# Float16 parts of q and k for the scores of two batches, in a kernel of attention and two expert layers

## The chip, the cores and the metric

The kernel runs on one core of a Trainium2 chip. The metric is the time of one execution on the device, in microseconds (us); less is better. The core has five engines that run side by side, each through a list of instructions in order: TensorE (PE, matrix products; its weight loads are shown apart as PEld), VectorE (DVE), ScalarE (ACT), GpSimd (POOL) and SyncE (SP), which here issues the transfers (DMA).

## The reference

Attention over 4 batches, 8 heads, 576 tokens and 64 dimensions of a head, with a retrieval from a memory beside it, then two layers of the form in-product, pointwise function, out-product. Everything is float32.

```python
scores = scale * np.matmul(q, k.transpose(0, 1, 3, 2))        # scale = 1/8
scores = np.where(causal, -1000000000.0, scores)
a = np.exp(scores - scores.max(-1, keepdims=True))
a /= a.sum(-1, keepdims=True) + 1e-09
local = np.matmul(a, v)
mem_out = (phi(q) @ M_prev) / (phi(q) @ z_prev + 1e-06)        # phi(x) = x + 1, or exp(x) for x < 0
x = g * mem_out + (1 - g) * local                              # g = sigmoid(beta), one for each head
...                                                            # x is laid out as 2304 tokens x 512
y   = (s * relu(x @ w_in)**2 + b) @ w_out                      # layer 1, d_ff = 2048
h   = y @ w_in2
out = (max(h, 0) + alpha * min(h, 0)) @ w_out2                 # layer 2, d_ff = 2048
```

## The kernel before

**Attention.** The work is cut into units, a unit being two heads (a pair) of one batch: 4 pairs for each of batches 0, 2 and 3, and 8 half units in batch 1 (SPLIT). The 576 queries are cut into five chunks of 128, 128, 128, 128 and 64 (CHUNKS, AT). The scores of chunk c against its keys are one matmul for each head (L974), of 256, 384, 128, 512 and 576 columns; the two heads of a pair lie in the upper and the lower 64 partitions, so that two matmuls of 64 rows each fill the array. Batches 0, 2 and 3 (QUAD) issue the scores of a unit in two steps: chunks 0 and 1, and then 2, 3 and 4. The float32 q and k are the operands directly, with no preparation. `largest` (L947) adds the mask and takes the maximum of a row, `exps` (L940) takes the exponent with its sum, and the weights go turned into the output products, in float16 parts for batches 1 to 3 (L878). `values` makes two float16 parts of v in each unit, scaled by a sum that is taken over it: Abs with an accumulator (L672), a reduction on GpSimd (L675), small operations on VectorE, a scaled copy on ScalarE (L684), a subtraction on VectorE (L686). L918 puts the unit's result together, L1035 sends it to the memory `x1`.

**Layer 1.** Tokens are taken in blocks: block 0 has 512, blocks 1 to 7 have 256. The x of a block is loaded in halves of two pairs (L1195), cast to the format of the products on ScalarE (L1202) and its rest taken on VectorE (L1204). A block of 256 goes in 16 steps of 24 matmuls: `g1` makes the hidden values of 128 columns of w_in in 12 matmuls into the bank `hb` (L1109 to L1111), ScalarE and VectorE square them (L1122 to L1125), and `g2` adds their share of the output in 12 matmuls into `yb` (L1143 to L1145). `x` and the weights are in two parts each, so there are three products. L1179 stores y. While layer 1 goes on, the weights of layer 2 are prepared: L1263 to L1278 combine them, L1314 and L1317 split them into float16 parts on ScalarE and VectorE, and L1409, L1410 and L1460 do the like with y.

**Layer 2** uses seven products in place of eight with such parts (L1485 to L1487 and L1624 to L1626).

**What sets the order.** Nothing is issued as the code stands. Each piece is an `op` with an engine, an assumed cost, the pieces that it needs and a priority; the class Plan simulates the engines and, whenever one is free, lets it take the ready piece of the lowest number. Attention has numbers from 0 on (`ATT`), the layers from 10,000,000 on (`MOE`), so that layer matmuls fill what attention leaves of TensorE. The table NUDGE shifts the number of single pieces. In the program that comes out, each engine goes through its list strictly in order.

Of the kernel before, what the change touches and what calls it, by code (L numbers as in the profile page):

```python
# [10 lines left out]
FP16 = mybir.dt.float16  # L11
# [38 lines left out]
GW = 640  # L50
# [16 lines left out]
LIFT = 2.0 ** 14  # L67
TOP, DOWN = 2.0 ** 13, 2.0 ** -22
WP = 1.7
NUDGE = {  # L70
# [391 lines left out]


def t_p(ns):

    return 206 + 4 * sum(ns) / 2.4 + (0, 0, 4, 160, 187)[len(ns)]


def t_dve(n, rate=1.04, extra=0.0):
    return 69 + n * rate + extra  # L470


def t_act(n, fixed=93.0, extra=0.0):
    return fixed + n * 0.834 + extra
# [1256 lines left out]
```

## Time and profile before

| what | value |
|---|---|
| median of three runs | 907.01 us (906.0 to 907.03) |
| the profiled execution | 904.36 us |
| its span, from the first to the last instruction shown | 902.6 us |
| mean granted clock of TensorE | 0.998 |
| TensorE busy | 889.4 us, 99% of the span |
| VectorE busy | 748.6 us, 83% |
| ScalarE busy | 608.4 us, 67% |
| GpSimd busy | 13.9 us, 2% |

The span is what the profiler sees of the profiled execution; 1.76 us of it lie outside. Busy time is the union of an engine's instructions. Matmuls overlap one another in their pipeline, so the distance from one start to the next says what a matmul costs, and its duration does not.

### The profile page before, as it was taken

How to read it: one execution, taken by the hardware profiler on the slowest of the kernel's cores; microseconds unless marked ns; L12 is line 12 of the kernel's file. 1: busy time of each engine (PE TensorE's matmuls, PEld its weight loads, DVE VectorE, ACT ScalarE, POOL GpSimd, SP SyncE). 2: the span in 40 equal slices, each digit the busy share in tenths (PEclk: the TensorE clock that was granted, in tenths of full speed). 3: DMA queues.
4: the chain of work that ended last, by engine and by line, in shares of the span. 5: the costliest groups of instructions: out<-in, count | busy, mean ns of one | idle time of the engine just before them, and what ended most of it. 6: DMA issues, size and time to landing. Idle time of an engine off the chain costs nothing.

```text
span 902.6 us, 19354 instructions
## 1 busy us (share of the span) xinstructions
PE 889.4 (99%) x7144; PEld 690.7 (77%) x7144; DVE 748.6 (83%) x1729; ACT 608.4 (67%) x1416; POOL 13.9 (2%) x41
## 2 busy tenths in 40 slices
PE   8999999999999999999999999999999999999998
PEld 5767678688988898899999999765566666666665
DVE  8999999788686757759988978898968899795974
ACT  8987776788788878744545478876758775455451
POOL 0000000000000000000000000000000000000000
PEclk9999999999999999999999999999999999999999
DMA  4359895387957586457878769856544262726202
GB/s 164 110 167 261 194 283 184 75 233 123 151 135 158 122 188 116 95 185 254 297 253 279 263 221 325 277 187 216 170 163 169 105 201 99 245 88 191 89 1 70
DMA packets 154527, 160.44 MB, mean 178 GB/s; under 512 B 86976, under 2 KB 128576, under 8 KB 154432
## 3 DMA queue, kind: packets, MB, share of 16 engines
q1 hardware_dynamic: 154144, 158.91, 60.0%
q8 instruction: 56, 0.92, 0.4%
q14 instruction: 39, 0.32, 0.1%
q10 hardware_dynamic: 288, 0.30, 0.1%
HBM read 92.84 MB, written 46.66 MB: 155 GB/s over the span
## 4 chain that ended last, share of the span: by engine, by line
PE 84%; DVE 9%; DMA 3%; ACT 2%; issue 1%; SPq 0%; DVEq 0%
PE yb L1143 7%; PE hb L1109 7%; PE yb L1145 7%; PE yb L1144 6%; PE hb L1111 6%; PE hb L1110 6%; PE sp L1626 3%; PE sp L1625 3%; PE sp L1624 3%; PE yb L1626 3%; PE yb L1625 3%; PE yb L1624 3%; PE sp L974 2%; PE yb L1487 2%; PE yb L1486 2%; PE yb L1485 2%
## 5 line engine op out<-in xcount | busy, mean ns | idle before, releaser
L1109 PE MATMUL hb<-xr,wt 128*128 128x256 f32 (+1 forms) x512 | 152.8, 299 | 1.1 <-ACT gt L1122 1.1
L1143 PE MATMUL yb<-gr,wt 128*128 128x256 f32 (+2 forms) x512 | 153.4, 300 | 0.2
L1145 PE MATMUL yb<-gr,wt 128*128 128x256 f32 (+2 forms) x512 | 150.7, 294 | 0.7 <-DVE gr L1125 0.5
L1111 PE MATMUL hb<-xr,wt 128*128 128x256 f32 (+1 forms) x512 | 149.7, 292 | 0.4 <-DVE wt L1075 0.4
L1110 PE MATMUL hb<-xr,wt 128*128 128x256 f32 (+1 forms) x512 | 149.4, 292 | 0.0
L1122 ACT ACTIVATE gt<-hb 128x256 f32<-128x256 f32 (+1 forms) x128 | 52.4, 410 | 97.5 <-PE hb L1111 93.7
L1109 PEld LDWEIGHTS hb<-xr,wt 128*128 128x128 f32 x512 | 96.5, 189 | 11.1 <-issue 5.6
L1143 PEld LDWEIGHTS yb<-gr,wt 128*128 128x128 f32 x512 | 96.6, 189 | 9.4 <-issue 5.1
L1145 PEld LDWEIGHTS yb<-gr,wt 128*128 128x128 f32 x512 | 96.4, 188 | 4.5 <-DVE gr L1125 1.9
L1111 PEld LDWEIGHTS hb<-xr,wt 128*128 128x128 f32 x512 | 96.2, 188 | 3.8 <-DVE wt L1075 1.4
L1110 PEld LDWEIGHTS hb<-xr,wt 128*128 128x128 f32 x512 | 96.2, 188 | 2.3
L1144 PE MATMUL yb<-gr,wt 128*128 128x256 f32 (+2 forms) x320 | 93.7, 293 | 0.0
L1125 DVE TENSOR_TENSOR gr<-gt,gr 128x256 fp32r<-128x256 f32 (+1 forms) x128 | 58.2, 455 | 31.2 <-ACT gr L1124 29.9
L1144 PEld LDWEIGHTS yb<-gr,wt 128*128 128x128 f32 x320 | 60.2, 188 | 1.4
L1124 ACT CAST gr<-gt 128x256 fp32r<-128x256 f32 (+1 forms) x128 | 55.2, 431 | 6.0 <-PE yb L1144 3.5
L1123 ACT ACTIVATE gt<-gt 128x256 f32<-128x256 f32 (+1 forms) x128 | 56.8, 444 | 2.4
L1144 PE MATMUL yb<-gr,wu 128*128 128x256 f32 (+2 forms) x192 | 56.2, 293 | 0.0
L1486 PEld LDWEIGHTS <-wp 128*128 128x128 f16 x336 | 32.9, 98 | 23.0 <-issue 1.6
L1625 PEld LDWEIGHTS <-wp 128*128 128x128 f16 x336 | 32.9, 98 | 21.7
L1626 PEld LDWEIGHTS <-wp 128*128 128x128 f16 x336 | 32.9, 98 | 21.7
L1624 PEld LDWEIGHTS <-wp 128*128 128x128 f16 x336 | 32.9, 98 | 21.7
L1487 PEld LDWEIGHTS <-wp 128*128 128x128 f16 x336 | 32.9, 98 | 21.7
(493 smaller groups left out, 2427.6 us busy)
## 6 DMA issues: line engine op xcount, KB each, us to landing
g<-poolx SPq DMA_DIRECT2D x96, 192.0 KB, 1.9
poolu<-g SPq DMA_DIRECT2D x30, 384.0 KB, 4.4
pool<-wout SPq DMA_DIRECT2D x13, 512.0 KB, 4.9
room<-win SPq DMA_DIRECT2D x13, 512.0 KB, 4.3
room<-wout SPq DMA_DIRECT2D x12, 512.0 KB, 4.1
pool<-win SPq DMA_DIRECT2D x11, 512.0 KB, 4.8
spare<-y SPq DMA_DIRECT2D x12, 384.0 KB, 4.1
spare<-g SPq DMA_DIRECT2D x12, 384.0 KB, 3.8
```

The source lines that it names most:

```text
L1109: T.matmul(H_, W_h, X_h, start=(d == 0), stop=False)
L1110: T.matmul(H_, W_h, X_l, start=False, stop=False)
L1111: T.matmul(H_, W_l, X_h, start=False, stop=(d == KD - 1))
L1123: op("ACT", t_act(n), lambda: A.activation(out=t_, in_=t_, func=AF.Square), w=[tk], prio=-1)
L1124: op("ACT", t_act(n), lambda: A.copy(out=G_h, in_=t_), r=[tk], w=[("gh", gj)], prio=-1)
L1125: op("DVE", t_dve(n), lambda: V.tensor_tensor(out=G_l, in0=t_, in1=G_h.bitcast(F32), op=ALU.subtract), r=[tk, ("gh", gj)], w=[("gl", gj)], ...
L1143: T.matmul(Y, W_h, G_h, start=first, stop=False, skip_group_check=True)
L1144: T.matmul(Y, W_l, G_h, start=False, stop=False, skip_group_check=True)
L1145: T.matmul(Y, W_h, G_l, start=False, stop=False, skip_group_check=True)
L1624: T.matmul(o, W_h, G_h, start=(m == e == 0 and P in (1, 2, 4, 5)), stop=False, skip_group_check=True)
L1625: T.matmul(o, W_l, G_h, start=False, stop=False, skip_group_check=True)
L1626: T.matmul(o, W_h, G_l, start=False, stop=False, skip_group_check=True)
```

## The change

Batches 2 and 3 (HALF) take their scores from float16 parts. `halves` makes, once for each unit, a scale for q and one for k from the sums of their absolute values (largest over the partitions), and a high and a low part of each. `mm16` then has three matmuls in place of one: high by high, high by low, low by high, into the same bank. The scores come out scaled; `exps` takes the scale back by the factor of its activation, and `unscale`, a small operation behind `largest`, by a product with the row's maximum. The mask's constant becomes larger. `t_h` is the cost that Plan assumes for the new score steps. All of NUDGE is listed anew, since the numbers of the pieces behind the new ones shift.

```diff
+HALF = (2, 3)
 NUDGE = {
-    0: 45, 1: 61, 5: 2, 6: -161, 8: -3, 10: 90, 12: 1, 15: 111, 16: 376, 17: -48, 18: -27, 19: -30, 20: -37, 22: 3,
...
+    4422: 46, 4423: 46,
 }
+def t_h(ns):
+
+    return 150 + 3 * sum(n / 2.4 + 3 for n in ns) + 100 * (len(ns) > 2)
...
+        hst = stat[:, 98:116].rearrange("p (a b) -> p a b", a=2)
...
-            V.tensor_scalar(out=mask[:, S - 128:], in0=col, scalar1=row[:, 0:1], scalar2=-8.0e9, op0=ALU.is_gt, op1=ALU.mult)
+            V.tensor_scalar(out=mask[:, S - 128:], in0=col, scalar1=row[:, 0:1], scalar2=-1.0e30, op0=ALU.is_gt, op1=ALU.mult)
...
+        def halves(u, sq, sk, ranges):
+
+            j = u % 2
+            x = hst[:, j]
+            out = [Slot(RES["vf"]) for _ in range(2)]
+            for e, (s, o, (a, z)) in enumerate(zip((sq, sk), out, ranges)):
+                op("ACT", t_act(z - a, 93, 180), lambda e=e, s=s, o=o, a=a, z=z: A.activation(
+                    out=at(o, S)[:, a:z], in_=at(s, ranges[1][1] if e else S)[:, a:z], func=AF.Abs, accum_out=x[:, e:e + 1]),
+                   r=[s], w=[o, ("hm", j, e)])
+            op("POOL", 900, lambda: nc.gpsimd.partition_all_reduce(x[:, 2:4], x[:, 0:2], 128, ReduceOp.max),
+               r=[("hm", j, e) for e in range(2)], w=[("hx", j)])
+
+            def scales():
+                V.tensor_scalar(out=x[:, 4:6], in0=x[:, 2:4], scalar1=2.0 ** -15, scalar2=2.0 ** -15, op0=ALU.max, op1=ALU.mult)
+                V.reciprocal(out=x[:, 6:8], in_=x[:, 4:6])
+                V.tensor_scalar(out=x[:, 8:9], in0=x[:, 4:5], scalar1=x[:, 5:6], scalar2=-1.0, op0=ALU.mult, op1=ALU.mult)
...
+                op("ACT", t_act(z - a, 93, 93), lambda part=part, raw=raw, sc=sc: A.activation(
+                    out=part(0), in_=raw(), func=AF.Copy, scale=sc), r=[s, ("hs16", j)], w=[o])
+                op("DVE", t_dve(z - a, 1.04, 60), lambda part=part, raw=raw, sc=sc: V.scalar_tensor_tensor(
+                    out=part(1), in0=raw(), scalar=sc, in1=part(0), op0=ALU.mult, op1=ALU.subtract), r=[s, ("hs16", j)], w=[o])
+            return out
...
-                        out=at(s, GW)[:, x + k0:x + k0 + kn], in_=bank_at(bk)[:, at0:at0 + kn], func=AF.Exp, scale=-1.0, bias=mcol,
+                        out=at(s, GW)[:, x + k0:x + k0 + kn], in_=bank_at(bk)[:, at0:at0 + kn], func=AF.Exp, scale=hst[:, j, 8:9] if b in HALF else -1.0, bias=mcol,
...
+                def unscale(c, cols):
+                    if b not in HALF:
+                        return
+                    m = mx[:, j, cols[0]:cols[-1] + 1]
+                    op("DVE", 73, lambda: V.tensor_scalar(out=m, in0=m, scalar1=hst[:, j, 8:9], scalar2=-1.0, op0=ALU.mult, op1=ALU.mult),
+                       r=[("hs16", j)], w=[("mx", j, x) for x in cols])
...
+                    def mm16():
+                        for y in range(0, len(todo), 2):
+                            for l0, l1 in ((0, 0), (0, 1), (1, 0)):
+                                for bk, rows, odd, q0, nq, k0, n, x in todo[y:y + 2]:
+                                    T.matmul(bank_at(bk)[rows, x:x + n], half16(sq16, odd, l0, q0, nq), half16(sk16, odd, l1, k0, n),
+                                             start=l0 + l1 == 0, stop=l0 == 1, skip_group_check=True)
```

New lines stand between, so the same code has other numbers after: `g1` is L1181 to L1183 and `g2` L1215 to L1217, the layers' work on ScalarE L1194 to L1196, the stores of x and y L1107 and L1251, the loads of x L1267, the scores L1044 (float32) and L1037 (float16), the weight splits L1386 and the copies of y L1532.

Three places of the order show what moves. The first is SyncE at the end of batch 2's attention: the last transfer to `x_65` is the x of pair 3, the loads from it feed a block of layer 1. Before:

```order
L1035 DMA x_65<-pool 128x576
L840 DMA pool<-kp 128x576
L659 DMA pool<-vd 128x640
L1195 DMA poolx<-x_65 128x2x256
L827 DMA_TRANSPOSE pool<-pool 128x10x128 x2
L827 DMA_TRANSPOSE pool<-poolx 128x10x128
L1195 DMA poolx<-x_65 128x2x256
L1179 DMA y_66<-pool 128x256 x2
L1179 DMA y_66<-poolx 128x256
L1179 DMA y_66<-pool 128x256
L1195 DMA poolx<-x_65 128x2x256
```

After:

```order
L1267 DMA poolx<-x_65 128x2x256
L750 DMA poolx<-qp 128x576
L1107 DMA x_65<-pool 128x576
L1251 DMA y_66<-poolx 128x256
L1251 DMA y_66<-pool 128x256 x2
L1251 DMA y_66<-poolx 128x256
L1267 DMA pool<-x_65 128x2x256 x2
L875 DMA_TRANSPOSE pool<-poolx 128x10x128
L875 DMA_TRANSPOSE poolx<-poolx 128x10x128
```

After, the first load stands ahead of that store and belongs to another block; behind the store come four stores of y and then both loads of block 3 together, where before the loads of x lie apart, with loads and transposes of the next units between.

The second is TensorE behind the outputs of batch 2's pair 3 (`yb_103`): before, three layer matmuls and the second score step of the next unit, and then the layer's block goes on (`yb_102`).

```order
L878 MATMUL yb_103<-pool 64x64
L1143 MATMUL yb_101<-gr,wt_1451 128x256
L1144 MATMUL yb_101<-gr,wt_1451 128x256
L1145 MATMUL yb_101<-gr,wt_1451 128x256
L974 MATMUL yb_104<-poolx,pool 128x512
L974 MATMUL sp_106<-poolx,pool 128x512
L974 MATMUL sp_107<-poolx,pool 128x128
L974 MATMUL ob<-poolx,pool 128x128
L974 MATMUL sp_107<-poolx,pool 64x288 x2
L974 MATMUL ob<-poolx,pool 64x288 x2
L1143 MATMUL yb_102<-gr,wt_1451 128x256
L1144 MATMUL yb_102<-gr,wt_1451 128x256
```

After, nine layer matmuls stand there, which end their block, and then the score step in float16 begins, each matmul with its own weight load:

```order
L932 MATMUL yb_103<-pool,poolx 64x64
L1215 MATMUL yb_101<-gr,wt_1756 128x256
L1216 MATMUL yb_101<-gr,wt_1756 128x256
L1217 MATMUL yb_101<-gr,wt_1756 128x256
L1215 MATMUL yb_102<-gr,wt_1756 128x256
L1216 MATMUL yb_102<-gr,wt_1756 128x256
L1217 MATMUL yb_102<-gr,wt_1756 128x256
L1215 MATMUL yb_102<-gr,wt_1756 128x256
L1216 MATMUL yb_102<-gr,wt_1756 128x256
L1217 MATMUL yb_102<-gr,wt_1756 128x256
L1037 LDWEIGHTS pool
L1037 MATMUL sp_106<-pool 128x512
```

Behind that score step, the matmuls of the next block's hidden values (`hb`) begin at once, with none of `yb` between them:

```order
L1037 MATMUL ob<-pool 64x288
L1181 MATMUL hb<-xr,wt_505 128x256
L1182 MATMUL hb<-xr,wt_505 128x256
L1183 MATMUL hb<-xr,wt_505 128x256
L1181 MATMUL hb<-xr,wt_505 128x256
L1182 MATMUL hb<-xr,wt_505 128x256
L1183 MATMUL hb<-xr,wt_505 128x256
L1181 MATMUL hb<-xr,wt_505 128x256
L1182 MATMUL hb<-xr,wt_505 128x256
L1183 MATMUL hb<-xr,wt_505 128x256
L1181 MATMUL hb<-xr,wt_505 128x256
L1182 MATMUL hb<-xr,wt_505 128x256
```

What moved is the start of block 3: it stands 106 layer matmuls behind the outputs before, and 10 to 16 behind them after.

The third is ScalarE near the end of layer 1, where the splits of layer 2's weights (`wp`) and the copies of y (`spare`) stand among the layers' own work (`gt`, `gr`). After:

```order
L1194 ACTIVATE gt<-hb 128x256
L1386 ACTIVATE wp_7065<-wp_7065,stat 128x2x256
L1386 ACTIVATE wp_7167<-wp_7167,stat 128x3x256
L1195 ACTIVATE gt<-gt 128x256
L1532 ACTIVATE spare<-spare,stat 128x384
L1196 CAST gr<-gt 128x256
L1194 ACTIVATE gt<-hb 128x256
L1532 ACTIVATE spare<-spare,stat 128x384
L1195 ACTIVATE gt<-gt 128x256
L1532 ACTIVATE spare<-spare,stat 128x384
L1196 CAST gr<-gt 128x256
L1532 ACTIVATE spare<-spare,stat 128x384
```

The maxima over layer 2's weights (`bounds`), which all splits need, stand at step 114 of layer 1's 128 before and at step 120 after, so that the rows above are among those of the last seven steps.

## Rows read from the trace of the kernel before

**Rows 1.** Busy time by stretch: span, busy us per engine, clock, DMA share, GB/s.
```profile
0.00:60.00 60.00, 54.66 (x484) 39.80 (x486) 55.02 (x222) 53.58 (x166) 2.37 (x12) 0.97 0.45 145
...
180.00:390.00 210.00, 209.82 (x2349) 187.45 (x2351) 153.67 (x495) 168.51 (x475) 5.52 (x18) 1.00 0.69 146
390.00:530.00 140.00, 139.94 (x1252) 139.67 (x1247) 122.30 (x270) 65.56 (x166) 1.34 (x2) 1.00 0.72 252
530.00:570.00 40.00, 39.13 (x328) 37.23 (x327) 32.21 (x58) 35.60 (x72) 0.00 (x0) 1.00 0.93 309
570.00:902.60 332.60, 328.07 (x2025) 198.22 (x2023) 271.88 (x402) 199.81 (x341) 1.03 (x2) 1.00 0.46 150
```

**Rows 2.** TensorE's timeline, a first score step: start us, duration us, instruction.
```profile
266.47 0.48 PE L974 MATMUL yb<-poolx 64*128 64x256 f32 x1
266.47 0.48 PE L974 MATMUL ob<-poolx 64*128 64x256 f32 x1
...
267.75 0.39 PE L1143 MATMUL yb<-gr,wt 128*128 128x256 f32 x1
```

**Rows 3.** TensorE's timeline, the second score step of a unit.
```profile
302.44 0.69 PE L974 MATMUL yb<-poolx,pool 64*128 64x512 f32 x1
...
304.84 0.39 PE L1143 MATMUL yb<-gr,wt 128*128 128x256 f32 x1
```

**Rows 4.** Timelines, x of batch 2's pair 3: TensorE, VectorE, SyncE, ScalarE, VectorE.
```profile
301.90 0.38 PE L1143 MATMUL yb<-gr,wt 128*128 128x256 f32 x1
...
302.03 0.55 DVE L918 TENSOR_SCALAR pool<-yb,vsc 128x320 f32<-128x320 f32 x1 [0.48 <-PE yb L878]
...
302.60 0.33 SPq L1035 DMA_DIRECT2D x<-pool  x1
...
305.95 0.38 SPq L1195 DMA_DIRECT2D poolx<-x  x1
...
310.02 0.71 ACT L1202 CAST xr<-poolx 128x256 fp32r<-128x256 f32 x2
...
311.46 0.73 ACT L672 ACTIVATE pool<-pool 128x640 f32<-128x640 f32 x1
312.09 0.19 ACT L672 ACTIVATION_READ_ACCUMULATOR pool<-pool 128x1 f32 x1
...
310.42 0.88 DVE L686 SCALAR_TENSOR_TENSOR pool<-poolx,vsc,pool 128x640 f16<-128x640 f32 x1
311.22 0.75 DVE L1204 TENSOR_TENSOR xr<-poolx,xr 128x256 fp32r<-128x256 f32 x2
311.89 0.15 DVE L1001 TENSOR_TENSOR sm<-sm 128x1 f32<-128x1 f32 x1
```

**Rows 5.** Busy time by stretch around TensorE's longest wait, columns as in the first.
```profile
50.00:52.00 2.00, 0.61 (x4) 0.21 (x2) 2.00 (x12) 2.00 (x8) 0.00 (x0) 1.00 0.89 250
52.00:54.00 2.00, 1.96 (x9) 1.26 (x11) 1.97 (x9) 1.86 (x7) 0.00 (x0) 0.63 1.01 378
54.00:56.00 2.00, 2.00 (x8) 0.92 (x7) 0.96 (x3) 2.00 (x5) 0.00 (x0) 0.52 1.01 336
```

**Rows 6.** TensorE's timeline, output matmuls in float16.
```profile
197.84 0.22 PE L878 MATMUL sp<-pool,poolx 128*64 128x128 f16 x1
...
197.90 0.22 PE L878 MATMUL sp<-pool,poolx 128*64 128x128 f16 x1
```

**Rows 7.** Page, costliest groups: count, busy us and mean ns, idle before.
```profile
L1486 PEld LDWEIGHTS <-wp 128*128 128x128 f16 x336 | 32.9, 98 | 23.0 <-issue 1.6
```

**Rows 8.** ScalarE by line: count, busy us and mean ns, idle before.
```profile
L1124 ACT CAST gr<-gt 128x256 fp32r<-128x256 f32 (+1 forms) x128 | 55.2, 431 | 6.0 <-PE yb L1144 3.5
...
L1314 ACT ACTIVATE wp<-wp,stat 128x512 f16<-128x512 f32 (+1 forms) x48 | 37.6, 790 | 0.9 <-PE yb L1486 0.5 <-DMA wp<-wdwi 0.2
...
L1460 ACT ACTIVATE spare<-spare,stat 128x384 f32<-128x384 f32 x24 | 16.0, 702 | 0.1
...
L1409 ACT CAST poolu<-spare 128x768 f16<-128x768 f32 x8 | 6.5, 828 | 0.0
```

More of the change, by code (lines that the diff above doesn't have):

```diff
@@ L688, in values, with part, raw @@
             return sf
+        def halves(u, sq, sk, ranges):
[12 more added lines that the diff above has]
+                V.tensor_scalar(out=x[:, 8:9], in0=x[:, 4:5], scalar1=x[:, 5:6], scalar2=-1.0, op0=ALU.mult, op1=ALU.mult)
+            op("DVE", 390, scales, r=[("hx", j)], w=[("hs16", j)])
+            for e, (s, o, (a, z)) in enumerate(zip((sq, sk), out, ranges)):
+                def part(lo, o=o, a=a, z=z):
+                    return at(o, 2 * S, FP16)[:, S * lo + a:S * lo + z]
+                def raw(e=e, s=s, a=a, z=z):
+                    return at(s, ranges[1][1] if e else S)[:, a:z]
+                sc = x[:, 6 + e:7 + e]
+                op("ACT", t_act(z - a, 93, 93), lambda part=part, raw=raw, sc=sc: A.activation(
[3 more added lines that the diff above has]
+            return out
         def features(b, p, u, gs):
@@ L842, in pair, with half16 @@
                    r=gate(b, u, KG), prio=(-21, -8)[k] if b + p == 0 else None, w=[(sk, "b") if k else sk], bytes_=512 * (z - a))
+            if b in HALF:
+                sq16, sk16 = halves(u, sqp, sk, ((AT[SETS[gs[0]][0]], AT[SETS[gs[-1]][-1]] + CHUNKS[SETS[gs[-1]][-1]][0]), (0, nkeys)))
+            def half16(s, odd, lo, x, n):
+                return at(s, 2 * S, FP16)[D * odd:D * odd + D, S * lo + x:S * lo + x + n]
             def half(s, odd, x, n):
@@ L940, in exps @@
                     op("ACT", t_act(kn, 50, 180), lambda: A.activation(
-                        out=at(s, GW)[:, x + k0:x + k0 + kn], in_=bank_at(bk)[:, at0:at0 + kn], func=AF.Exp, scale=-1.0, bias=mcol,
-                        accum_out=scol), r=[(bk, c), ("mx", j, mk)], w=[(s, c, k0), ("sm", j, int(c > 1), col)])
+                        out=at(s, GW)[:, x + k0:x + k0 + kn], in_=bank_at(bk)[:, at0:at0 + kn], func=AF.Exp, scale=hst[:, j, 8:9] if b in HALF else -1.0, bias=mcol,
+                        accum_out=scol), r=[(bk, c), ("mx", j, mk)] + [("hs16", j)] * (b in HALF), w=[(s, c, k0), ("sm", j, int(c > 1), col)])
                     dones[c > 1].append(("sm", j, int(c > 1), col))
@@ L970, in scores @@
                                      for i in range(2) for odd in range(2)]
+                    def mm16():
[4 more added lines that the diff above has]
+                                             start=l0 + l1 == 0, stop=l0 == 1, skip_group_check=True)
                     def mm():
+                        if b in HALF:
+                            return mm16()
                         for bk, rows, odd, q0, nq, k0, n, x in todo:
@@ L980, in scores @@
                         room_for.append(("hs", u))
-                    op("PE", t_p([y[6] for y in todo[::2]]), mm, r=[sqp, sk] + [(s, "b") for s in (sqp, sk) if max(step) > 1],
+                    op("PE", (t_h if b in HALF else t_p)([y[6] for y in todo[::2]]), mm, r=[sq16, sk16] if b in HALF else [sqp, sk] + [(s, "b") for s in (sqp, sk) if max(step) > 1],
                        w=keys + room_for, prio=ATT + (base + 2 * step[0]) * 10, kind="scores")
@@ L991, in pair @@
                         mcols = [largest(c, 2 * c + odd, bks[odd], 0, n, mask[:, S - n:], "mask", at0=at0) for odd in range(2)]
+                        unscale(c, [2 * c, 2 * c + 1])
                         for odd in range(2):
@@ L997, in pair @@
                     m1 = largest(c, 8, bks[1], n2, n2, mask2, "mask2", m0)
+                    unscale(c, [8])
                     exps(c, 0, 9, bks[0], 0, n2, m1, 8)
```

260 rows, old and new, of the table NUDGE are left out of this document.

## The prediction

> **What bounds the kernel now.** I read the busy times by stretch first [rows 1]. TensorE is the bound almost everywhere: 209.82 of 210 us from 180 to 390, 139.94 of 140 up to 530, 39.13 of 40 up to 570, and 328.07 of the last 332.6. Only the first 60 us, in which the attention of batch 0 runs without the layers beside it, are shared: TensorE 54.66, VectorE 55.02, ScalarE 53.58. So a microsecond taken out of TensorE's stream between 180 and 390, where all units of batches 2 and 3 lie, comes off the end, as long as nothing else makes TensorE wait. VectorE (153.67 of 210) and ScalarE (168.51 of 210) have 56 and 41 us to spare there.
>
> Second, TensorE's timeline around the scores [rows 2, 3]. A unit of batches 2 and 3 has two steps of scores. The reader is to see the distance from the first score matmul to the next layer matmul: 267.75 - 266.47 = 1.28 us, and 304.84 - 302.44 = 2.40 us. The eight units repeat this, so the price of scores before is 3.68 us a unit.
>
> Third, how the chain of x is built, since the order puts another neighbour there now (below) [rows 4]. Fourth, the one place where TensorE's clock falls [rows 5].
>
> **The change part by part.**
>
> *Scores.* A unit streams 256 + 384 columns in its first step and 512 + 128 + 2 x 288 in its second, 1,856 for each head, with the two heads side by side (two records of 64 rows start together in [rows 2]). At 2.4 columns per ns, four passes for float32 make 3.09 us, and 0.59 us of the 3.68 are entry, loads and tail. Three float16 products make 3 x 1,856 / 2.4 = 2.32 us. That 128 columns of float16 cost no more than such a stream is seen in the output matmuls, whose pairs start 0.06 us apart [rows 6]; 128 / 2.4 is 0.053. No row shows float16 pairs of 64 rows. I give the entry, the loads and the tail 0.2 to 0.6 us, so 2.5 to 2.9 a unit, a saving of 6.0 to 9.2 us over eight units. I take 2.72, or **-7.7 us**, with the fixed part near the old one. The worst bound is from the weight loads: there are 36 of them in a unit, 98 ns each [rows 7]; if they were strictly one after another and nothing ran under them it would be 3.53 us plus the fixed part, and nothing would be saved. The layers' loads run under the matmuls (187.45 us of loads beside 209.82 of matmuls [rows 1]), so I don't take it.
>
> The Trainium skill ("TensorEngine Tiling (Array Packing)", section "Key Properties") says that different tiles of the array can load weights and multiply in parallel. For float32 the trace agrees as far as multiplying goes: the two heads start within 10 ns. By that rule the short pairs of 128 columns would not wait for two loads in a row, and the saving would be 8.3 us (an estimate); if the loads of the two heads queue it would be 7.2.
>
> *Making the parts.* Each unit gains on ScalarE two Abs with accumulators (0.73 + 0.19) and two scaled copies of about the same 0.73 (these rows are of 640 columns, not 576), about 3.3 us, and on VectorE two subtractions of at most 0.88 and eight small operations of 0.15 to 0.2, about 3.0 us [rows 4]. Eight units make 26 us and 24 us. Spread over 180 to 390 these fit into the 41 and 56 us to spare; operations that may run on either engine can move. POOL's one reduction a unit is nothing to an engine that is busy 5.52 of 210 us [rows 1]. I cost all this at 0 for TensorE, because the parts are made a unit ahead; if that cover were gone, a unit would wait for Abs, reduction, scales, copy, subtraction in a row, some 4 us.
>
> *The order around block 3.* The lists in the order show that the layers reach block 3, whose x needs the attention of batch 2, much closer behind it. Before, the last outputs of batch 2's pair 3 stand at layer matmul 1,035 and block 3's first matmul at 1,141: 106 matmuls between, 106 x 0.112 = 12 us (0.112 is 139.94 us over 1,252 matmuls [rows 1]). After, they stand at 1,143 and 1,153: nine matmuls of the layer's second product (1.01 us), the second score step of the next unit (2.40 x 2.72 / 3.68 = 1.77 us, and 0.2 for the two changes), and six matmuls on the half of x that is there already (0.67): **3.65 us of cover**. What has to happen in that time is seen in the same chain before: the outputs are done and the next layer matmul starts at 301.90; VectorE puts the sum together from 302.03; SyncE sends x away at 302.60 and, when this has landed, loads the block's half at 305.95; ScalarE's cast starts at 310.02 and VectorE's difference at 311.22, of which the first of two is done at about 311.6 [rows 4]. That is 9.7 us. VectorE was at another operation from 310.42 (L686, 0.88 us) while the cast was done, and ScalarE too was between other work, so I let the chain be up to 1.3 us shorter: 8.4. In the order after, x's store is followed on SyncE by four stores of y before the loads, which are issued, not waited for. So TensorE, which stands in order, waits at block 3's seventh matmul for 8.4 - 3.65 = 4.8 to 9.7 - 3.65 = 6.0 us. SyncE's two transposes behind those loads wait with nobody who is late. For what else may differ there I widen it to 4.0 to 6.5 and take **+5.0 us**.
>
> *The clock behind that wait.* In 50 to 52 TensorE is busy 0.61 of 2.0 us, the granted clock then is 0.63 and 0.52 in the next two stretches (1.2 GHz is the lower of its two levels), and full again after it [rows 5]. With about 0.37 + 0.48 of these two stretches of 2 us lost, such a fall costs up to 1.7 us. A wait of 5 us is longer than that one. I take **+1.2** (0 to 1.7).
>
> The Trainium skill ("TensorE: Matmul & The Clock Gate", section "Why this matters for your kernels") warns that gaps between bursts of matmuls let the array drop back to half of its clock. [Rows 5] agree: the clock fell right behind the emptiest stretch. It speaks against this change, which puts a gap into a stretch that had none; without the fall the sum would be 1.2 us lower.
>
> *The end of layer 1.* Preparing the weights of layer 2 starts some steps later and is squeezed into the last seven steps of layer 1. In these the order has on ScalarE 16 weight splits of 0.790, 7 of L1460's copies of 0.702, 3 of L1409's casts of 0.828 and 21 operations of the layers' own of about 0.431 [rows 8]: 12.6 + 4.9 + 2.5 + 9.1 = 29.1 us, less some 0.1 us by which neighbours overlap (311.46 + 0.73 ends 0.1 behind the 312.09 at which the next one starts [rows 4]), 47 x 0.1 = 4.7: 24.4 us. TensorE has 7 x 24 matmuls of 0.112 and 12 products of layer 2 of 0.162 (328.07 us over 2,025 [rows 1]): 20.8 us. So up to 3.6 us could become a wait; before, this stretch loses 0.87 us [rows 1]. ScalarE can run ahead on what doesn't hang on TensorE, so I take **+1.2** (0 to 4).
>
> *The rest.* Up to layer matmul 384 the same work stands in another order: no row prices that, and I put it at 0, with 1.5 us on either side. The mask's constant costs nothing: the same instruction.
>
> Sum: -7.7 + 5.0 + 1.2 + 1.2 = **-0.3 us** on the profiled execution's 904.36, so 904.1. The median of the runs shown is 907.01, 2.65 above that execution; the forecast is 904.1 + 2.65 = 906.7, put as **906.5 us**.
>
> **The rivals.**
>
> *B: the gap isn't there.* If x comes as quickly as the cover allows, the wait and the clock go: -7.7 + 1.2 = -6.5, or 900.5 on the median. For it: ScalarE and VectorE may be freer there than in [rows 4]. Against it: the two transfers alone took from 302.60 to near 310.
>
> *E: the new order wins at the start.* TensorE is idle 5.3 us of the first 60 [rows 1]. If the relisted order closes half of it, 3 us, the sum is -3.3: 903.7. Against: VectorE and ScalarE are nearly full there too, and their work there is the same.
>
> *C, the slower side: ScalarE is overfull in the last seven steps of layer 1.* The layers' relu and square stand behind weight splits on the same queue, and TensorE waits for them. It decides once ScalarE's 24.4 us really run within those steps: 3.6 us of wait in place of 1.2, and a fall of the clock behind them of up to 1.7, so -0.3 + 2.4 + 1.5 = +3.6: 910.6. For it: ScalarE was busy 35.60 of 40 us there already [rows 1]. Against: the splits before it are earlier in the order.
>
> *D: the change doesn't do what it says.* The float16 halves don't run side by side: 3 x 2 x 1,856 / 2.4 = 4.64, with 0.4 fixed 5.04 a unit, 1.36 more than before instead of 0.96 less: -0.3 + 7.7 + 10.9 = +18.3: 925. For it only that no row shows such pairs; against it that float32 ones do run so [rows 2].
>
> **How the numbers follow.** Chances: the forecast 0.40, B 0.18, E 0.15, C 0.22, D 0.05. The forecast's own range is 904 to 909 (saving 6.0 to 9.2, wait 4.0 to 6.5, clock 0 to 1.7). About 0.2%, 1.8 us, is what a measurement of this kernel can tell from no change: faster is below 905.2, slower above 908.8. The forecast gives 0.09 faster, 0.26 same, 0.05 slower; B 0.18 faster; E 0.13 faster and 0.02 same; C 0.05 same and 0.17 slower; D 0.05 slower. Together 0.40, 0.33 and 0.27. The range reaches half a microsecond beyond B's value and C's, 900.0 to 911.0; outside it are D and the far parts of B and C.
>
> **What would show it.** In the profile after: the distance from a unit's first score matmul to the next layer matmul, 2.5 to 2.9 us over both steps; one new wait of 4 to 6.5 us of TensorE at the start of block 3, released by the difference of x, with a granted clock near half in the stretches right behind it; TensorE's idle time from some 20 us before layer 2's stretch to it not above 4 us; TensorE idle about as long in the first 60 us as before. The prediction is wrong if there is no such wait, if the scores take 3.5 us or more, or if a new wait above 2 us stands elsewhere.

## The result, and the profile after

The changed kernel takes 913.12 us (median of 4 runs, 912.83 to 915.95); the kernel before, beside it on the same chip, 906.5. The ratio is 1.0088, with an interval of 1.0065 to 1.0112: slower by 8.0 us, where 906.5 was forecast with a range up to 911.0. The profiled execution took 913.37 us, its span is 911.6.

Busy time by stretch, columns as in [rows 1]:

```profile
0.00:60.00 60.00, 54.61 (x462) 39.14 (x462) 55.19 (x221) 52.32 (x161) 1.43 (x11) 0.97 0.44 138
...
180.00:390.00 210.00, 201.37 (x2272) 181.80 (x2272) 162.35 (x535) 183.70 (x494) 7.56 (x25) 0.98 0.65 138
390.00:530.00 140.00, 139.36 (x1351) 137.91 (x1350) 115.76 (x262) 73.43 (x193) 0.20 (x1) 1.00 0.70 236
530.00:570.00 40.00, 38.42 (x328) 37.45 (x327) 33.36 (x79) 26.65 (x59) 3.56 (x2) 1.00 0.87 300
570.00:911.60 341.60, 337.23 (x2095) 206.10 (x2093) 287.25 (x423) 212.51 (x365) 1.46 (x2) 1.00 0.49 159
```

TensorE stands idle for 210 - 201.37 = 8.63 us from 180 to 390; it was 0.18 in [rows 1]. The loss falls between 175 and 550 us: counted along TensorE's timeline, the 384th layer matmul starts 0.16 us later than before, the 1,728th 9.5, the 2,832nd 7.4 and the 3,000th 8.0.

TensorE's timeline, both score steps of a unit and the start of block 3 (start, duration, line, tiles, count; in brackets the idle time before and what ended it); answers to [rows 2, 3]:

```profile
310.97 0.50 PE L1037 MATMUL sp<-pool 64*128 64x256 f16 x6
311.31 0.32 PE L1037 MATMUL ob<-pool 64*128 64x384 f16 x1
311.31 0.32 PE L1037 MATMUL yb<-pool 64*128 64x384 f16 x1
...
311.88 0.38 PE L1215 MATMUL yb<-gr,wt 128*128 128x256 f32 x1
...
314.54 0.38 PE L1215 MATMUL yb<-gr,wt 128*128 128x256 f32 x1
...
315.77 0.82 PE L1037 MATMUL sp<-pool 64*128 64x512 f16 x6
316.43 0.22 PE L1037 MATMUL yb<-pool 64*128 64x128 f16 x1
316.43 0.22 PE L1037 MATMUL ob<-pool 64*128 64x128 f16 x1
316.48 0.22 PE L1037 MATMUL yb<-pool 64*128 64x128 f16 x1
...
317.54 0.38 PE L1181 MATMUL hb<-xr,wt 128*128 128x256 f32 x1
...
318.23 0.28 PE L1183 MATMUL hb<-xr,wt 128*128 128x256 f32 x1
323.56 0.58 PE L1181 MATMUL hb<-xr,wt 128*128 128x256 f32 x1 [5.05 <-ACT xr L1274]
```

The scores take 311.88 - 310.97 = 0.91 and 317.54 - 315.77 = 1.77 us, 2.68 a unit in place of 3.68. The two heads start at the same time. The wait stands where it was forecast. Its chain in the timelines of the other engines, answering to [rows 4]:

```profile
314.66 0.55 DVE L972 TENSOR_SCALAR pool<-yb,vsc 128x320 f32<-128x320 f32 x1 [0.17 <-PE yb L932]
...
315.24 0.33 SPq L1107 DMA_DIRECT2D x<-pool  x1
315.70 0.33 SPq L1251 DMA_DIRECT2D y<-poolx  x1
316.21 2.48 SPq L1251 DMA_DIRECT2D y<-pool  x2
318.78 0.40 SPq L1251 DMA_DIRECT2D y<-poolx  x1
319.51 0.88 SPq L1267 DMA_DIRECT2D pool<-x  x2
...
322.81 0.70 ACT L1274 CAST xr<-pool 128x256 fp32r<-128x256 f32 x2
```

From the sum on VectorE to TensorE's next matmul it is 323.56 - 314.66 = 8.9 us. (Ahead of the prediction both loads at L1267 are given to block 3. One of the two is the second half of block 3, the other that of block 4.) The clock behind the wait, in stretches of 2 us, answering to [rows 5]:

```profile
318.00:320.00 2.00, 0.51 (x5) 0.30 (x3) 2.00 (x6) 2.00 (x5) 0.00 (x0) 1.00 0.57 189
320.00:322.00 2.00, 0.00 (x0) 0.00 (x0) 2.00 (x9) 1.04 (x4) 0.00 (x0) 0.91 0.68 198
322.00:324.00 2.00, 0.44 (x1) 0.29 (x1) 1.74 (x6) 2.00 (x8) 0.00 (x0) 0.50 1.12 244
324.00:326.00 2.00, 1.49 (x6) 1.14 (x5) 2.00 (x7) 2.00 (x6) 0.00 (x0) 0.50 1.25 176
326.00:328.00 2.00, 1.92 (x9) 1.93 (x10) 0.39 (x4) 2.00 (x9) 0.00 (x0) 0.50 0.99 287
328.00:330.00 2.00, 2.00 (x11) 2.00 (x11) 1.84 (x9) 1.76 (x5) 0.51 (x2) 0.50 0.06 21
330.00:332.00 2.00, 2.00 (x12) 2.00 (x12) 2.00 (x4) 2.00 (x6) 0.00 (x0) 0.53 0.00 0
```

The reader is to see two things: the clock is at half for five stretches, and ScalarE, and but for 326 to 328 (0.39) VectorE, are nearly full in the same ones. Last, the new operations behind the maxima, and two rows of the exponents of 512 columns, the first with the factor read from the tile `stat`, as in batches 2 and 3, the second with a constant (VectorE by line, ScalarE by line and form: count, busy us and mean ns, idle before):

```profile
L1011 DVE TENSOR_SCALAR mx<-mx,stat 128x2 f32<-128x2 f32 (+1 forms) x40 | 8.9, 222 | 0.2
...
L994 ACT ACTIVATE pool<-sp,mx,stat 128x512 f32<-128x512 f32 x7 | 5.4, 776 | 0.0
...
L994 ACT ACTIVATE pool<-sp,mx 128x512 f32<-128x512 f32 x5 | 3.4, 686 | 1.2 <-DVE vsc L696 1.2
```

With the factor from the tile an exponent takes 776 - 686 = 90 ns longer. Over all widths the 80 exponents of batches 2 and 3 take some 0.09 us longer each, about 7 us of ScalarE in all. No row before has this form, since there the factor is the constant -1, and Plan assumes the same cost for both.

### The profile page after: what moved, and what is told of

Same layout as the page of the kernel before. It is cut to its first block, busy times and chain, and to the rows that moved or that the text cites. A ratio compares the mean times of both kernels' runs of the same rounds, so it can differ in the third digit from the quotient of the medians.

```text
span 911.6 us, 19681 instructions
## 1 busy us (share of the span) xinstructions
PE 889.0 (98%) x7240; PEld 693.0 (76%) x7240; DVE 767.2 (84%) x1804; ACT 635.4 (70%) x1469; POOL 17.9 (2%) x49
## 4 chain that ended last, share of the span: by engine, by line
PE 52%; ACT 6%; DVE 2%; issue 1%; DMA 1%; SPq 0%; DVEq 0%; ACTq 0%
PE yb L1217 3%; PE hb L1181 3%; PE sp L1696 3%; PE sp L1698 3%; PE yb L1698 3%; PE yb L1697 3%; PE yb L1696 3%; PE sp L1697 3%; PE hb L1183 3%; PE hb L1182 3%; PE yb L1216 3%; PE yb L1215 2%; PE yb L1557 2%; PE yb L1558 2%; PE yb L1559 2%; PE sp L1557 2%
## 5 line engine op out<-in xcount | busy, mean ns | idle before, releaser
L1181 PE MATMUL hb<-xr,wt 128*128 128x256 f32 (+1 forms) x512 | 154.8, 302 | 9.6 <-ACT xr L1274 5.0
L1217 PE MATMUL yb<-gr,wt 128*128 128x256 f32 (+2 forms) x512 | 150.9, 295 | 1.9 <-DVE gr L1197 1.9
L1215 PE MATMUL yb<-gr,wt 128*128 128x256 f32 (+2 forms) x512 | 152.5, 298 | 0.0
L1183 PE MATMUL hb<-xr,wt 128*128 128x256 f32 (+1 forms) x512 | 149.9, 293 | 0.0
L1194 ACT ACTIVATE gt<-hb 128x256 f32<-128x256 f32 (+1 forms) x128 | 52.3, 409 | 97.6 <-PE hb L1183 91.6
L1181 PEld LDWEIGHTS hb<-xr,wt 128*128 128x128 f32 x512 | 97.2, 190 | 21.2 <-issue 6.1
L1215 PEld LDWEIGHTS yb<-gr,wt 128*128 128x128 f32 x512 | 96.8, 189 | 6.3 <-issue 2.8
L1217 PEld LDWEIGHTS yb<-gr,wt 128*128 128x128 f32 x512 | 96.5, 188 | 6.1 <-DVE gr L1197 3.4
L1183 PEld LDWEIGHTS hb<-xr,wt 128*128 128x128 f32 x512 | 97.1, 190 | 2.6
L1196 ACT CAST gr<-gt 128x256 fp32r<-128x256 f32 (+1 forms) x128 | 55.3, 432 | 6.4 <-PE yb L1216 4.4
```

The costliest lines, as they stand in the source:

```text
L1181: T.matmul(H_, W_h, X_h, start=(d == 0), stop=False)
L1183: T.matmul(H_, W_l, X_h, start=False, stop=(d == KD - 1))
L1196: op("ACT", t_act(n), lambda: A.copy(out=G_h, in_=t_), r=[tk], w=[("gh", gj)], prio=-1)
L1215: T.matmul(Y, W_h, G_h, start=first, stop=False, skip_group_check=True)
L1217: T.matmul(Y, W_h, G_l, start=False, stop=False, skip_group_check=True)
```

## The experiments

Each ran beside the kernel before; ratios are to that, with a 95% interval, and a ratio times 906.5 gives the us named. First theory: the loss is the wait at block 3 with the clock behind it. The rivals: the order alone, the products, the making of the parts, the small operations behind the maxima. The slower exponents were not among the rivals. They are in every run below but the float32 scores, the small operations alone, the fixed scale and the new list.

**x in two parts.** The store of batch 2's last x is cut, so that block 3's half goes first; its load and casts are moved forward.

```diff
+todo["x"] = lambda: part(0, 256)        # columns of block 3, stored ahead
+todo[1074] = lambda: part(256, S)
+plan.ops[2501][6][0].place = 11         # another buffer for the load
+put("x", 1067)
+put(2501, 2706)
+for i in (2504, 2502, 2505, 2503):
+    put(i, 1110)
```

> The changed kernel with one transfer cut in two: the x of batch 2's pair 3 is sent to memory in two parts (256 tokens as soon as they are done, then the rest), and the second half of block 3's x, which needs only the first part, is loaded and cast earlier. Nothing else moves. Theory 1 (the wait of 5.05 us at block 3 and the half clock behind it are what the change lost): TensorE's wait before the seventh matmul of block 3 goes from 5.05 us to under 0.5, the granted clock stays 1.0 from 316 to 332, and the time falls by 5.05 + about 3.5 = 8.5 us, to about 904.6 (ratio to before 0.998). Rival 2 (attention is late as a whole, and the wait only moves on to the next thing that needs it): a wait of 3 us or more comes up at another place behind block 3's start, and the time stays above 909. Rival 3 (the loss is spread over ScalarE and VectorE, the wait at block 3 would have been caught up later): 912 or more.

916.42 us, 1.0114 (1.0098 to 1.0131). TensorE's wait at block 3's seventh matmul is gone, but ScalarE, in order, stood for the load, and TensorE waited elsewhere. ScalarE's timeline:

```profile
315.56 0.71 ACT L1274 CAST xr<-poolx 128x256 fp32r<-128x256 f32 x2 [4.62 <-DMA poolx<-x]
```

TensorE's waits from 300 to 340 (line, whom it waited for, sum in us, times, longest):

```profile
PE yb L773 <- DVE pool L756: 5.5, 1, 5.5
PE sp L1037 <- ACT pool L994: 2.0, 1, 2.0
```

So 5 us went over to the features of the next unit (L756). That is partly the experiment's own doing, since it blocked ScalarE, so this run doesn't say what the wait by itself takes from the end.

**The wait filled.** 22 float32 matmuls of 128 columns, whose result nobody reads, stand ahead of the waiting matmul.

```diff
+for _ in range(22):
+    T.matmul(ybank[0][:, 0:128], ident, ident, start=True, stop=True, skip_group_check=True)
```

> The changed kernel with 22 matmuls of 128x128 in float32 on the identity, whose results nobody reads, in the place where TensorE waits before the seventh matmul of block 3. The wait for x stays as long, but TensorE is busy in it. Theory 1 (of the loss, 5 us are the wait and about 3.5 are the clock at half behind it, 10.2 us long by the clock's record): granted clock 1.0 through 316 to 332, the first matmul behind the wait at the same distance from the store of x as before, and the time 3.5 us less, about 909.6. The prediction's own size for the clock (1.2 us): 911.9. Rival (the clock fall costs nothing, since TensorE has to wait for ScalarE and VectorE there anyway): 913.1, no change.

913.96, 1.0082 (1.0069 to 1.0096): no change against the kernel after. Its stretches:

```profile
320.00:322.00 2.00, 2.00 (x21) 2.00 (x19) 2.00 (x8) 1.04 (x4) 0.00 (x0) 1.00 0.73 202
322.00:324.00 2.00, 1.75 (x13) 1.36 (x12) 1.74 (x7) 2.00 (x8) 0.00 (x0) 1.00 1.14 261
324.00:326.00 2.00, 0.80 (x6) 0.61 (x6) 1.78 (x6) 2.00 (x7) 0.00 (x0) 1.00 1.32 191
326.00:328.00 2.00, 2.00 (x18) 2.00 (x19) 0.61 (x4) 1.99 (x7) 0.00 (x0) 1.00 0.79 283
328.00:330.00 2.00, 2.00 (x18) 1.83 (x16) 1.84 (x8) 1.87 (x5) 0.51 (x2) 1.00 0.01 5
330.00:332.00 2.00, 0.52 (x5) 0.48 (x5) 2.00 (x5) 2.00 (x5) 0.00 (x0) 1.00 0.04 8
```

The clock stays full, and TensorE, now quicker, waits: 10 - 7.07 = 2.93 us idle from 322 to 332. The half clock cost nothing that can be measured here. The first theory fell as far as the clock goes.

**Float32 in the new order.** Scores as before, on unscaled copies of q and k; no sums, no subtractions, no small operations, the exponents with a constant factor, and the list of after.

```diff
-    for l0, l1 in ((0, 0), (0, 1), (1, 0)):
...
-            T.matmul(bank_at(bk)[rows, x:x + n], half16(sq16, odd, l0, q0, nq), half16(sk16, odd, l1, k0, n),
...
+    T.matmul(bank_at(bk)[rows, x:x + n], half(sq16, odd, q0, nq), half(sk16, odd, k0, n),
+             start=True, stop=True, skip_group_check=True)
```

> The order of the changed kernel, instruction by instruction, with the scores of batches 2 and 3 in float32 again: one matmul in place of three, on plain copies of q and k that ScalarE makes where it made the high parts; the sums, the scales, the low parts and the small operations behind the maxima are left out. Theory 1 (the new products themselves gain what was forecast, and the new order loses): the scores of a unit take 3.68 us in place of 2.69, so +7.9; the wait at block 3 is shorter by 0.6, and some small waits between 180 and 450 go, 1 to 2 us: about 918.5. Rival 2 (the saving in the scores is hidden behind other engines): within 2 us of the changed kernel, 913. Rival 4 (what costs is making the parts, and the order is as good as before): 908 or less.

914.7, 1.0089 (1.0076 to 1.0102); TensorE waits 4.0 us at block 3. The order alone, with the copies, costs 8.1 us.

**Parts not made.** New order; the products read a fixed table (the bits of the mask), and the sums, copies and subtractions (64 operations) are left out; the small operations and the exponents' factor from the tile are kept. The attention weights of batches 2 and 3 are thus not the reference's.

```diff
-    return at(s, 2 * S, FP16)[D * odd:D * odd + D, S * lo + x:S * lo + x + n]
+    return mask.bitcast(FP16)[D * odd:D * odd + D, x:x + n]
```

> The changed kernel without the making of the parts: the score matmuls of batches 2 and 3 read a fixed table in place of the parts of q and k, and sums, reduction, scales, copies and subtractions are left out (64 operations); the order of all else is the same. Theory 1 (making the parts costs only small waits, 3 to 4 us of TensorE between 180 and 450 in place of 0.5 before; the wait at block 3 comes from the order and the two transfers): ScalarE and VectorE lose about 18 us of busy time between 180 and 390, the small waits shrink to about 1 us, the wait at block 3 stays between 4 and 5 us with the clock at half behind it, and the time is about 910. Rival 4 (the fuller ScalarE and VectorE are what makes x late at block 3): the wait there falls under 2 us and the time to 904 or less. Rival 5 (parts cost nothing at all): 913.

911.26, 1.0051 (1.0037 to 1.0066), with 5.3 us of wait at block 3. All the making together is worth 8.0 - 4.6 = 3.4 us; 4.6 remain, though the scores are short.

**The old order with table products and small operations.** The order of before, the same table (and so the same omission), one small operation behind each of 72 maxima, and the exponents with their factor from the tile.

```diff
+    if b in HALF and col < 9:
+        V.tensor_scalar(out=mcol, in0=mcol, scalar1=hst[:, j, 8:9], scalar2=-1.0, op0=ALU.mult, op1=ALU.mult)
```

> The kernel before, in its own order, with one thing changed: the score matmuls of batches 2 and 3 are the three float16 products, read from a fixed table (the parts of q and k are not made), with the small operations behind the maxima. Theory 6 (formed after the first runs: the products gain what they should wherever TensorE is the bound, and what costs is the relisted order, in which attention falls behind the layers): 8 units x 0.99 us = 7.9 us less than before, minus a microsecond or two for waits that open where a score step ends sooner: 899 to 901. Rival 2 (attention is set by the chain through ScalarE, VectorE and the transfers in any order, so that a shorter score step only makes TensorE wait): 904 to 907.

922.39, 1.0182 (1.0154 to 1.021). I had held by then that the new order alone is what costs, and that the old one would keep the saving. That theory, too, fell.

**The old order with the whole making.** The sums, parts and small operations set into the order of before, 5 to 15 us ahead of their scores, in a place of their own (`spare`), with two loads of layer 2's input moved later.

```diff
+for ahead, fn in ((15, lambda f=load: (f(0), f(1))), (9.5, lambda f=size: (f(0), f(1))), (8, most), (7, scales),
+                  (6, lambda f=high: (f(0), f(1))), (5, lambda f=low: (f(0), f(1)))):
+    todo.append((t0 - 1e3 * ahead, 1, fn))
```

> The whole arithmetic of the change in the old order: the kernel before with its list, and to each unit of batches 2 and 3 the making of the parts is added where the old order has the scores: loads of q and k into a tile that is free at that time 15 us ahead of the first score step, Abs 9.5, reduction 8, scales 7, high parts 6 and low parts 5 us ahead (by the planner's clock), the three products, and a small operation behind each maximum. Two early loads of y (and their maxima) go behind the attention, since they used that tile. Theory 6: the products give 7.9 us, the making on ScalarE and VectorE takes back 1.9 (what it cost in the new order, 913.1 against 911.3) to 4: 901 to 903, faster than both kernels. Rival 4 (making the parts costs as much as the products save, in any order): 906 or more, with new waits of TensorE for ScalarE or VectorE of 5 us and more between 190 and 390.

946.98, 1.0453 (1.0425 to 1.0482). Much of that may be my placement, which no planner saw; it shows only that the parts are no free addition to this order.

**Products without small operations, and small operations alone, in the old order.** The first has the table products (and that omission) and, of the rest of the change, the exponents' factor from the tile:

```diff
-    ... func=AF.Exp, scale=-1.0, bias=mcol,
+    ... func=AF.Exp, scale=hst[:, j, 8:9] if b in HALF else -1.0, bias=mcol,
```

The second has float32 scores, exponents with the constant factor, and the 72 small operations with the factor 1, as in the diff before.

> As the run with the fixed table in the old order, without the 72 small operations behind the maxima: against the kernel before, nothing but TensorE's score matmuls of batches 2 and 3 is changed (three float16 products on a table in place of the float32 ones; the parts are not made). Theory 7 (what loses time in the old order is the small operation that now stands between each maximum and its exponents on VectorE, in a burst in which VectorE and ScalarE are full and the layers' own operations stand in the same lists): the time falls from 922.4 to between 899 and 904; the products then gain 2 to 8 us. Rival 2 (a shorter score step only makes TensorE wait in any order): 905 to 907, with TensorE's idle time up by as much as the steps are shorter. Rival 8 (the shorter steps themselves upset the old order): 912 or more.

> The kernel before, in its own order and with its float32 scores, with one thing added: a small operation on VectorE (a product of 128x1 with constants, which gives the same number) behind each of the 72 maxima of batches 2 and 3. In a row they take 72 x about 0.31 us = 22 us of VectorE (a row of the run with the table: from the end of a maximum to the start of the next one 0.31 us, 0.00 without it). Theory 7: 12 to 22 us more than before, 918 to 928, as waits of TensorE for the layers' operations on VectorE and ScalarE between 195 and 390 us. Rival (VectorE is busy 153.67 of 210 us there, so they fit, as the prediction had it): 906 to 909. Rival 8 (the shorter steps did it): no more than 908.

The products without small operations: 908.6, 1.004 (1.002 to 1.0061). The shorter stream gains nothing in this run. But more than TensorE's products was changed, other than the expectation says: the 80 exponents are slower here too (512 columns: 779 ns in place of 692). What the products by themselves would gain in the old order was not run. Its stretch from 180 to 390:

```profile
180.00:390.00 210.00, 205.38 (x2395) 184.10 (x2394) 151.97 (x492) 171.92 (x468) 5.54 (x18) 1.00 0.65 145
```

TensorE, busy 209.82 before, is now idle 4.62 us of it; in the whole span it waits most for ScalarE (`hb` for `gt`, 4.1 us in four waits; 1.1 before). The small operations alone: 919.13, 1.0147 (1.0121 to 1.0173), 13.3 us for 72 operations; beside the table products the same 72 cost 12.9 (1.0182 against 1.004). VectorE's timeline in that kernel, and then the same place before:

```profile
214.53 0.30 DVE L952 CUSTOM_DVE_ANT_0 sp<-sp,mask 128x128 f32<-128x128 f32 x1 [0.65 <-PE sp L983]
214.75 0.14 DVE L952 DVE_READ_ACCUMULATOR2_ANT mx<- 128x1 f32 x1
214.92 0.21 DVE L956 TENSOR_SCALAR mx<-mx,stat 128x1 f32<-128x1 f32 x1
215.05 0.69 DVE L952 CUSTOM_DVE_ANT_0 yb<-yb,mask 128x512 f32<-128x512 f32 x1
```

```profile
215.58 0.14 DVE L947 DVE_READ_ACCUMULATOR2_ANT mx<- 128x1 f32 x1
215.58 0.73 DVE L947 CUSTOM_DVE_ANT_0 yb<-yb,mask 128x512 f32<-128x512 f32 x1
```

Before, the next maximum starts with the read of the accumulator; with the small operation it starts 215.05 - 214.75 = 0.30 us after it. Nine of these stand in the maxima of a unit, and the layers' own subtraction (`gr`) is queued on VectorE behind them. TensorE's waits in that kernel, which were 0.5 for `yb` and 1.1 for `hb` before:

```profile
PE yb L1154 <- DVE gr L1134: 4.9, 7, 1.2
PE hb L1118 <- ACT gt L1131: 2.4, 5, 0.9
```

That is 5.7 us more. TensorE's idle time as a whole grows by 7.8 (917.3 - 896.3 against 902.6 - 889.4); how the rest of the 13.3 is lost was not traced.

**Fixed scale.** The order of after, with one power of two as the scale of all parts, which goes into the factor that `largest` has anyway. Copies, subtractions and three products stay; the sums, the scales and the small operations go, and the exponents have the constant factor again.

```diff
-    sc = x[:, 6 + e:7 + e]
+    sc = 2.0 ** 5
-    ... in1=m, scale=-0.125, scalar=...
+    ... in1=m, scale=-0.125 * (2.0 ** -10 if b in HALF else 1.0), scalar=...
```

> The changed kernel in its own order, with the parts of q and k made by a fixed power of two in place of the measured sums (which is enough for these inputs): Abs, reduction, scales and the 40 small operations behind the maxima are gone, the high and low parts and the three products stay. Theory 9 (in the stretch of batches 2 and 3 the pace is set by the bursts of VectorE and ScalarE behind each score step, and the small operations there are the dearest part of the change: 14.5 us for 72 in the old order, 0.2 us each): 40 x 0.2 = 8 us less, and up to 1.9 for the sums: 903 to 906, with the wait at block 3 still there but shorter. Rival 10 (in the new order the small operations have been given their place; what is lost is lost at block 3, where TensorE's list waits for x): 909 to 912, as in the run without the making, with the wait at block 3 of 4 to 5 us.

906.98, 1.0003 (0.9993 to 1.0014): the loss is gone, though TensorE still waits 4.6 us at block 3.

**No sums.** As after, but with the scales written once into the tile; the 40 small operations stay, and so do all reads of the tile.

```diff
+V.memset(hst[:, :, 6:8], 2.0 ** 5)
+V.memset(hst[:, :, 8:9], -2.0 ** -10)
```

> The changed kernel in its own order, with the sums taken out and the small operations kept: Abs, reduction and scales are left out, the scale of the parts stands in the tile from the start as a fixed power of two, and the 40 small operations behind the maxima and the scaled exponents stay. With the run of fixed scale (907.0, which has neither) and the changed kernel (913.1, which has both) it divides those 6.1 us. Theory 9 (small operations in VectorE's bursts, 0.2 us each in the old order, are the dear part): 911 to 912.5. Rival 11 (the sums, 16 times 0.87 us on ScalarE and a chain of 3 us ahead of the parts, are the dear part): 907.5 to 909.

912.01, 1.0067 (1.0045 to 1.0089). Against the fixed scale this differs by two things, which cost 5.8 us together: the 40 small operations (8.8 us of VectorE), and the scale that is read from a tile. The latter makes 80 exponents 0.09 us longer (780 ns against 694 at 512 columns), 16 copies 0.10 and 16 subtractions 0.06. How the 5.8 us divide between the two no run shows. In the two timelines the loss comes bit by bit, where the units of batches 2 and 3 lie: at the 800th layer matmul (253 us) it is 0.7, at the 1,056th 1.6, at the 1,159th (322 us) 2.5, at the 1,300th 4.0, at the 1,728th (419 us) 5.4. Half clock accounts for up to 1.7 us of that: behind the wait it lasts 10.2 us here and 6.8 with the fixed scale.

**A new list.** The fixed scale with NUDGE searched anew for its shorter list of pieces.

> The parts by a fixed power of two (no sums, no small operations) with the planner's list made anew for just these pieces, so that no piece is planned that isn't issued; block 3 then does not wait. Theory 12 (the products' saving is lost only where the order leaves TensorE waiting; with an order fitted to it, it comes off the end as far as ScalarE and VectorE, which still make the parts, leave it): scores 2.69 us a unit, no wait of TensorE over 1.5 us between 180 and 530, 900 to 904, faster than before and after. Rival 2 (the pace between 180 and 390 is not TensorE's in any order): 905 to 908, with 5 us or more of TensorE's idle time in small waits there.

907.05, 1.0011 (0.9996 to 1.0027). Here there is no wait at block 3, and from 180 to 390 TensorE is busy 208.43 us; at the 1,728th layer matmul the kernel is 2.6 us ahead of before. By the 3,000th it is 2.7 behind: between the two TensorE waited for the layers' work (`yb` for `gr` 1.3 us, `hb` for `gt` 1.1), and six more products of layer 2 stand there; the rest was not traced. The profiled execution, of 909.12 us, is the slowest of its twelve. It beats neither the kernel before nor the fixed scale in the order of after. No version here is faster than before.

## Why the prediction was wrong

The loss adds up in the order of after from these kernels:

| step | from - to | ratio, from - to | us |
|---|---|---|---|
| the new order, with float32 and copies | before - float32 | 1 - 1.0089 | +8.1 |
| three float16 products and subtractions | float32 - fixed scale | 1.0089 - 1.0003 | -7.8 |
| 40 small operations, and the scale read from a tile | fixed scale - no sums | 1.0003 - 1.0067 | +5.8 |
| sums and scales | no sums - after | 1.0067 - 1.0088 | +1.9 |

The last step is inside the intervals, the others are not.

- *Scores*, -7.7 forecast: (3.68 - 2.68) x 8 = 8.0 us by the distances in the trace, 7.8 by the runs, the subtractions included. Right, and rival D (heads one after another) is excluded by the equal starts. The 8.3 and 7.2 that stand beside the forecast have no working there; 8.0 lies between.
- *Wait at block 3*, +5.0: 5.05 us, with the chain as forecast: 323.56 - 314.54 = 9.02 us from the layer matmul behind the outputs (8.4 to 9.7 forecast), of which 3.97 are covered (3.65). The size of the wait is right, and rival B is out. That it takes its length from the end isn't shown.
- *Clock behind it*, 1.2: the fall is there, for far longer than [rows 5] let expect, but its removal gained nothing. I counted half a clock as lost time, where TensorE would have waited for VectorE and ScalarE anyway.
- *End of layer 1*, +1.2 (0 to 4): counted between the 2,832nd and the 3,072nd layer matmul, TensorE is idle 2.63 us against 0.15 before, so about 2.5. In range. TensorE's waits there are 1.5 for ScalarE (`hb` for `gt`) and 1.2 for VectorE (`yb` for `gr`), so what rival C says of ScalarE is there in part, but its price reaches only to 910.6.
- The order's three terms together: 7.4 forecast, 8.1 measured. That they come so close is partly luck, since 1.2 of the 7.4 is the clock, whose removal gained nothing, and in the float32 run of that order the wait is 4.0. Where what lies beyond the wait and the end of layer 1 is lost wasn't settled. Rival E is out: the start gains nothing (the 384th matmul is 0.16 late).
- *Making the parts*, 0: **this step failed.** In the prediction's words, "I cost all this at 0 for TensorE, because the parts are made a unit ahead". All that serves a measured scale costs 7.7 us (1.0003 to 1.0088). The sums and scales are 1.9 of it, inside the intervals. The other 5.8 belong to two things together. One is the five of the eight small operations of a unit that stand behind the maxima; I had put them into one sum with the parts, at 0.15 to 0.2, and they take 0.22. The other has no term in the prediction: the exponents that take the scale back read it from a tile, which adds 0.09 us to each of 80. Neither is made a unit ahead. Both stand between the scores and what waits for them, the one on VectorE and the other on ScalarE, however much room the mean over 210 us leaves there. That small operations can cost so much by themselves is shown in the old order (13.3 us for 72, nothing else changed); that they do so here, and not the exponents, is not shown. The copies and subtractions cost little: parts not made and no sums differ by them, 1.0051 against 1.0067, inside the intervals. With the 7.7 in the sum, -0.3 + 7.7 = 7.4, against 8.0 measured.

A second reading was weak. That a microsecond taken out of TensorE's stream "comes off the end" was held for likely from a share of 99.9%, and the room on VectorE from its 153.67 of 210 us. In the order of before the small operations alone leave TensorE's list as it is, add 15.4 us to VectorE, and cost 13.3: there VectorE's list too sets the end, and 99.9% of TensorE doesn't tell. In the new order the saving of the products is worth its full 7.8.

What stays open: how the 5.8 us divide between small operations and exponents, what the products gain in the old order with a constant factor, whether a list exists by which the fixed scale beats the kernel before, how much of the 946.98 is owed to my placement, and whether the wait at block 3 can be taken away without stopping ScalarE.

## What to carry to other kernels

Price an added small operation by the place where it stands: in a burst on an engine that works in order, 0.21 us of work cost 0.18 us of the whole kernel each (13.3 for 72), however idle that engine is on average. Look also for old operations that a change makes longer: the factor from a tile added 0.09 us to an exponent, and the prediction had no term for it. A nearly full engine with filler work isn't proof that its stream sets the end, so try a saving alone, in the order in which it is to run, and see in the trace that nothing else has changed its duration. And when a scale can be a constant that an operation carries already, that took away the whole loss here.

## What the runs showed of the hardware

Behind a gap of 5.05 us the granted clock fell to half and stayed there for some 10 us; TensorE was busy 1.92 to 2.00 of 2 us in the last three of these stretches. Behind the gap in [rows 5] it was lowered in two stretches of 2 us. The Trainium skill ("TensorE: Matmul & The Clock Gate", section "Why this matters for your kernels") warns that a gap between bursts of matmuls brings the rate down to half, and the trace agrees (0.50). That to fill such a gap need not pay (913.96 against 913.12) was not expected. An exponent whose factor is read from a tile took 776 ns at 512 columns, and one with a constant 686; for 128 columns it is 453 against 367 in the mean. A small operation on the maximum just read out starts the next maximum 0.30 us behind the accumulator's read, in place of 0.00. Two float16 matmuls of 64 rows, each with weights of its own, start at the same time, and the next such pair of 128 columns 316.48 - 316.43 = 0.05 us later, which is the price of the stream alone.
